# Attention decode and a gated MLP on one core: the scheduler's program against one written out by hand, with 48 KB rows, GpSimd folds and a late output projection

## The chip, the core and the metric

One Trainium2 chip, one of its cores. The metric is device time in microseconds, the median of the runs. The core has TensorE (PE), VectorE (DVE), ScalarE (ACT), GpSimd (POOL) and SyncE (SP), which here only issues DMAs, and 16 DMA engines between HBM and the on-chip memory.

## The reference

One token goes through a layer with a cache of 8192 keys: layernorm, queries of 32 heads of 192, softmax over the scores against K, the sum over V, the output projection, a residual; then layernorm, a gated MLP with ReLU on the gate, and a second residual. All is float32. K and V are 201 MB each, and every element is used once.

```python
q = (layernorm(x) @ wq).reshape(32, 192)             # x: 640
scores = einsum("hd,hkd->hk", q, k_cache) * 192**-0.5  # k_cache: 32 x 8192 x 192
o = einsum("hk,hkd->hd", softmax(scores), v_cache)
h = x + o.reshape(6144) @ wo                          # wo: 6144 x 640
y = layernorm(h)
gate, up = y @ W_gate, y @ W_up                       # 640 x 1536 each
out = h + (gate * (gate > 0) * up) @ W_down           # 1536 x 640
```

## The kernel before, in words

The program is written against a scheduling layer with pools: buffers rotate, and the layer inserts each wait. Every engine still runs its own instructions in the order of the code. SP issues all the large loads, in that order, and a load that must wait for its buffer holds up every load behind it.

- Tiles. The pool `kv` has six buffers of 24 KB per partition (`kv_t`). A head's K (or V) is two of them: `load_kv` (L82) reads half a head, 4096 keys, 32 keys to a partition, one row of 24 KB per partition. At the start five of the buffers hold the slabs of wq, at the end they hold the weights of the MLP.
- Queries. The slabs of wq are multiplied as they land (L159); the result `q4` holds 8 heads side by side on four partitions. `query` (L168) picks one head with the matrix `sel` and spreads it over 128 partitions, in PSUM.
- Scores (`scores_of`). For each 16 keys per partition DVE multiplies K by q in place (L178). DVE sums 10 of the 16 products of 192 (L179), and ACT the other 6, one by one, with an accumulating copy (L181).
- Softmax (`softmax_of`). The maximum goes over PE twice (L189, L193), ACT takes the exponential (L198), PE the sum (L200), DVE its reciprocal.
- Values (`values_of`). 32 matmuls per head (L217), two keys of each partition at a time; they go to four quarters of the output in turn. PE starts on a half as soon as it landed. `ob` (L220) is the scaled copy.
- Output projection. `wo` comes in nine groups (`load_wo`, L90), for four heads each and at the end two: `to_columns` (L232, L235) turns `ob` into columns `oT`, and `output_of` (L241) multiplies the group's rows of wo into the accumulator `acc`, which already holds x.
- Order. The loop at the end of the attention loads K of head h+1 and V of head h in halves, by turns, and issues the scores of h+1 behind the values of h.
- Tail. Behind the last head the weights up, gate and down are loaded in eleven DMAs (L283 to L290), in buffers that K and V left. h, its layernorm, the two projections (`project`, L319), the product and the down projection (L337) follow; the last DMA writes 640 numbers.

Of the kernel before, what the change touches and what calls it, by code (L numbers as in the profile page):

```python
# [1 line left out]

# [5 lines left out]
F32 = mybir.dt.float32  # L8
AF = mybir.ActivationFunctionType
ALU = mybir.AluOpType  # L10
AX = mybir.AxisListType


@with_exitstack
def kernel(
    ctx: ExitStack,
    tc: tile.TileContext,
    x: bass.AP,
    kc: bass.AP,
    vc: bass.AP,  # L20
    wq: bass.AP,
    wo: bass.AP,
    w_gate: bass.AP,
    w_up: bass.AP,
    w_down: bass.AP,
    out: bass.AP,
):
    nc = tc.nc
# [29 lines left out]
    ps_q = ctx.enter_context(tc.tile_pool(name="ps_q", bufs=2, space=bass.MemoryType.PSUM))
    ps_x = ctx.enter_context(tc.tile_pool(name="ps_x", bufs=1, space=bass.MemoryType.PSUM))
    ps_o = ctx.enter_context(tc.tile_pool(name="ps_o", bufs=1, space=bass.MemoryType.PSUM))  # L60
    ps_s = ctx.enter_context(tc.tile_pool(name="ps_s", bufs=2, space=bass.MemoryType.PSUM))
    ps_a = ctx.enter_context(tc.tile_pool(name="ps_a", bufs=1, space=bass.MemoryType.PSUM))

    xT = const.tile([P, DJ], F32, name="xT")
    xrow = const.tile([1, D], F32, name="xrow")
    nc.scalar.dma_start(xT, x[0, 0].rearrange("(p j) -> p j", p=P))
    nc.scalar.dma_start(xrow, x[0])


    wq_v = wq.rearrange("(p j) n -> p j n", p=P)  # L70
    wq_ts = []
    for j in range(DJ):
        t = kv.tile([P, TW], F32, name="kv_t")
        nc.sync.dma_start(t, wq_v[:, j, :])
        wq_ts.append(t)

    def load_kv(src, h, c, parts=1):
        t = kv.tile([P, TW], F32, name="kv_t")
        v = src[h, c * P * R:(c + 1) * P * R, :].rearrange("(p r) d -> p (r d)", p=P)
        n = TW // parts  # L80
        for i in range(parts):
            nc.sync.dma_start(t[:, i * n:(i + 1) * n], v[:, i * n:(i + 1) * n])  # L82
        return t

    def load_wo(gi):
        hs = GROUPS[gi]
        j = len(hs) * DH // P
        t = wts.tile([P, j, D], F32, tag="wo_t", name="wo_t")
        r0 = hs[0] * DH
        nc.sync.dma_start(t, wo[r0:r0 + len(hs) * DH, :].rearrange("(p j) n -> p j n", p=P))  # L90
        return t

    ones = const.tile([P, P], F32, name="ones")
    nc.vector.memset(ones, 1.0)
    eps = const.tile([P, 1], F32, name="eps")
    nc.vector.memset(eps, EPS)
    ident = const.tile([P, P], F32, name="ident")
    from concourse.masks import make_identity
    make_identity(nc, ident)

    sel = const.tile([P, NQ, P], F32, name="sel")
    nc.gpsimd.memset(sel, 0.0)
    for g in range(NQ):
        nc.gpsimd.memset(sel[g * Q:g * Q + 1, g, :], 1.0)

    par = const.tile([P, 2, Q], F32, name="par")
    for i in range(2):
        nc.vector.reduce_sum(par[:, i, 0:1], ident.rearrange("p (g c) -> p g c", c=Q)[:, :, i], axis=AX.X)
        nc.vector.tensor_copy(par[:, i, 1:Q], par[:, i, 0:1].to_broadcast([P, Q - 1]))

    def rstd_of(dst, var, name):

        ve = const.tile([P, 1], F32, name=f"ve{name}")
        nc.vector.tensor_scalar_add(ve, var, EPS)
        sd = const.tile([P, 1], F32, name=f"sd{name}")
        nc.scalar.activation(sd, var, AF.Sqrt, bias=eps)
        y = const.tile([P, 1], F32, name=f"y{name}")
        nc.vector.reciprocal(y, sd)
        t = const.tile([P, 1], F32, name=f"t{name}")
        nc.vector.scalar_tensor_tensor(t, y, ve, y, op0=ALU.mult, op1=ALU.mult)  # L120
        nc.vector.tensor_scalar(t, t, -0.5, 1.5, op0=ALU.mult, op1=ALU.add)
        nc.vector.tensor_mul(dst, y, t)


    s1 = const.tile([P, 1], F32, name="s1")
    nc.vector.reduce_sum(s1, xT, axis=AX.X)
    pm = ps_s.tile([P, 512], F32, name="ps_small")
    nc.tensor.matmul(pm[:, 0:1], ones, s1, start=True, stop=True)
    mean = const.tile([P, 1], F32, name="mean")
# [78 lines left out]
    for po in pos:  # L208
        nc.vector.memset(po, 0.0)
# [159 lines left out]
```

## Time and profile before

| | before |
|---|---|
| median of 3 runs | 1054.98 us (1054.37 to 1055.05) |
| span of the profiled execution | 1052.8 us; it has no other time of its own |
| read from HBM | 445.91 MB, 424 GB/s over the span |
| busy: PE, DVE, ACT, POOL | 438.6, 727.2, 325.1, 1.9 us |
| DMA engines, queue of SP | 99.1% of 16 engines' span, 22472 packets |
| chain that ended last | DMA 65%, DVE 25%, PE 8% |

A time in a view is counted from the span's start. The rows of a timeline give start, length, engine, line and operation, and in brackets the idle time ahead and what ended it. A matmul in float32 stands as two instructions in the trace.

### The profile page before, as it was taken

How to read it: one execution, taken by the hardware profiler on the slowest of the kernel's cores; microseconds unless marked ns; L12 is line 12 of the kernel's file. 1: busy time of each engine (PE TensorE's matmuls, PEld its weight loads, DVE VectorE, ACT ScalarE, POOL GpSimd, SP SyncE). 2: the span in 40 equal slices, each digit the busy share in tenths (PEclk: the TensorE clock that was granted, in tenths of full speed). 3: DMA queues.
4: the chain of work that ended last, by engine and by line, in shares of the span. 5: the costliest groups of instructions: out<-in, count | busy, mean ns of one | idle time of the engine just before them, and what ended most of it. 6: DMA issues, size and time to landing. Idle time of an engine off the chain costs nothing.

```text
span 1052.8 us, 8858 instructions
## 1 busy us (share of the span) xinstructions
PE 438.6 (42%) x3136; PEld 136.1 (13%) x3136; DVE 727.2 (69%) x418; ACT 325.1 (31%) x1676; POOL 1.9 (0%) x11
## 2 busy tenths in 40 slices
PE   3423444344444333433442444344335334432466
PEld 1101111111111010111110111111101111110122
DVE  1188877677867777687776778677876877777641
ACT  0143333223323332232232333233322322333230
POOL 0000000000000000000000000000000000000000
PEclk9756666666666666766666665766667666666667
DMA  9999999999999999999999999999999999999996
GB/s 394 429 429 431 431 427 430 429 431 431 430 430 427 431 430 428 432 429 429 432 430 430 429 430 430 427 431 430 430 425 433 431 430 430 429 430 429 428 421 247
DMA packets 22662, 446.48 MB, mean 424 GB/s; under 512 B 2645, under 2 KB 2649, under 8 KB 4442
## 3 DMA queue, kind: packets, MB, share of 16 engines
q1 hardware_dynamic: 22472, 445.92, 99.1%
q8 instruction: 24, 0.39, 0.2%
q14 instruction: 20, 0.16, 0.0%
q10 hardware_dynamic: 146, 0.01, 0.0%
HBM read 445.91 MB, written 0.00 MB: 424 GB/s over the span
## 4 chain that ended last, share of the span: by engine, by line
DMA 65%; DVE 25%; PE 8%; ACT 1%; issue 1%; SPq 0%
DMA kv_t<-in_A_k_cache_dram 53%; DVE kv_t L178 18%; DMA kv_t<-in_A_v_cache_dram 8%; DVE sc L179 6%; PE po L217 5%; DMA dn_a<-in_B_W_down_dram 2%; DMA kv_t<-in_A_wq_dram 2%; PE q L168 1%; PE ps_small L232 1%; ACT p L198 0%; PE qp L159 0%; PE ps_small L193 0%; PE ps_small L200 0%; DVE oT L235 0%; PE pd L337 0%
## 5 line engine op out<-in xcount | busy, mean ns | idle before, releaser
L178 DVE TENSOR_TENSOR kv_t<-kv_t,q 128x3072 f32<-128x3072 f32 x128 | 423.4, 3349 | 163.4 <-DMA kv_t<-in_A_k_cache_dram 163.0
L181 ACT ACTIVATE kv_t<-kv_t 128x192 f32<-128x192 f32 x768 | 267.6, 349 | 529.5 <-DVE kv_t L178 529.5
L217 PE MATMUL po<-kv_t,p 128*2 128x384 f32 x2048 | 296.0, 747 | 245.6 <-DMA kv_t<-in_A_v_cache_dram 245.6
L179 DVE TENSOR_REDUCE sc<-kv_t 128x10 f32<-128x1920 f32 x128 | 269.1, 2144 | 0.0
L168 PE MATMUL q<-q,sel 128*128 128x192 f32 x64 | 31.0, 589 | 290.4 <-DVE kv_t L178 290.4
L181 ACT ACTIVATION_READ_ACCUMULATOR kv_t<-kv_t 128x1 f32 x768 | 143.3, 187 | 0.0
L217 PEld LDWEIGHTS po<-kv_t,p 128*2 128x2 f32 x2048 | 60.3, 111 | 449.8 <-DMA kv_t<-in_A_v_cache_dram 271.4
L168 PEld LDWEIGHTS q<-q,sel 128*128 128x128 f32 x64 | 15.7, 303 | 319.4 <-DVE kv_t L178 243.0
L220 ACT ACTIVATE ob<-po,rl 128x384 f32<-128x384 f32 x32 | 18.6, 580 | 113.5 <-PE po L217 113.5
L202 DVE RECIPROCAL rl<-ps_small 128x1 f32<-128x1 f32 x32 | 5.4, 168 | 52.6 <-PE ps_small L200 52.6
L191 DVE TENSOR_REDUCE m<-ps_small 1x1 f32<-1x128 f32 x32 | 8.9, 279 | 42.3 <-PE ps_small L189 42.3
L235 DVE STREAM_TRANSPOSE oT<-ps_small 32x192 f32<-32x192 f32 (+1 forms) x32 | 11.8, 367 | 27.1 <-PE ps_small L232 27.1
L232 PE MATMUL ps_small<-ob,par 128*32 128x192 f32 (+1 forms) x144 | 25.7, 315 | 0.7 <-ACT ob L220 0.7
L159 PE MATMUL qp<-kv_t,xn 128*32 128x512 f32 x120 | 19.4, 801 | 10.1 <-DMA kv_t<-in_A_wq_dram 9.1
L200 PE MATMUL ps_small<-rs,ones 128*128 128x1 f32 x64 | 12.4, 264 | 24.9 <-ACT p L198 24.9
L241 PE MATMUL acc<-wo_t,oT 128*32 128x160 f32 (+1 forms) x408 | 19.9, 352 | 4.6 <-DVE oT L235 4.6
L193 PE MATMUL ps_small<-m,ones 1*128 1x1 f32 x64 | 12.3, 259 | 11.9 <-DVE m L191 11.9
L241 PEld LDWEIGHTS acc<-wo_t,oT 128*32 128x32 f32 (+1 forms) x408 | 14.0, 127 | 9.9 <-DVE oT L235 7.8
L200 PEld LDWEIGHTS ps_small<-rs,ones 128*128 128x128 f32 x64 | 9.7, 191 | 27.6 <-ACT p L198 27.6
L193 PEld LDWEIGHTS ps_small<-m,ones 1*128 1x128 f32 x64 | 9.6, 186 | 18.3 <-DVE m L191 18.3
L232 PEld LDWEIGHTS ps_small<-ob,par 128*32 128x32 f32 x144 | 11.3, 109 | 4.8 <-ACT ob L220 1.4
L198 ACT ACTIVATE p<-sc,nb 128x64 f32<-128x64 f32 x32 | 11.1, 348 | 1.2 <-ACT nb L195 0.2
(77 smaller groups left out, 79.9 us busy)
## 6 DMA issues: line engine op xcount, KB each, us to landing
kv_t<-in_A_k_cache_dram SPq DMA_DIRECT2D x64, 3072.0 KB, 33.7
kv_t<-in_A_v_cache_dram SPq DMA_DIRECT2D x63, 3072.0 KB, 39.7
kv_t<-in_A_wq_dram SPq DMA_DIRECT2D x5, 3072.0 KB, 20.7
wo_t<-in_A_wo_dram SPq DMA_DIRECT2D x7, 1920.0 KB, 43.0
kv_t<-in_A_v_cache_dram SPq DMA_DIRECT2D x4, 768.0 KB, 38.3
up_a<-in_B_W_up_dram SPq DMA_DIRECT2D x1, 3072.0 KB, 33.9
gt_a<-in_B_W_gate_dram SPq DMA_DIRECT2D x2, 1536.0 KB, 24.2
wo_t<-in_A_wo_dram SPq DMA_DIRECT2D x2, 960.0 KB, 41.4
```

Of the source, the lines that this page charges most:

```text
L159: nc.tensor.matmul(qps[b][g * Q:(g + 1) * Q, :], xn[:, j:j + 1].to_broadcast([P, Q]), wq_ts[j][:, c0:c0 + QB], start=(j == 0), stop=(j == ...
L168: nc.tensor.matmul(q[:, 0:DH], sel[:, g, :], q4[:, i * DH:(i + 1) * DH], start=True, stop=True)
L178: nc.vector.tensor_mul(ks, ks, q[:, None, :].to_broadcast([P, SUB, DH]))
L179: nc.vector.reduce_sum(sc[:, i0:i0 + SUB - NA], ks[:, :SUB - NA, :], axis=AX.X)
L181: nc.scalar.activation(ks[:, r, :], ks[:, r, :], AF.Copy, accum_out=sc[:, i0 + r:i0 + r + 1])
L193: nc.tensor.matmul(pb[:, 0:1], ones[0:1, :], m1, start=True, stop=True)
L200: nc.tensor.matmul(pl[:, 0:1], ones, rs, start=True, stop=True)
L217: nc.tensor.matmul(po[g * Q:g * Q + 2, :], p[:, 2 * i:2 * i + 2], vts[c][:, r * DH:(r + 2) * DH], start=(i < NQ), stop=(i >= NP - NQ))
L220: nc.scalar.activation(ob, po, AF.Copy, scale=rl)
L232: nc.tensor.matmul(pt[q0:q0 + Q, 0:W], par[:, k, :], ob[:, k * DH + u * W:k * DH + (u + 1) * W], start=(k == 0), stop=(k == 1))
L235: nc.vector.transpose(oT[s], pt[s, 0:W].rearrange("p (c j) -> p j c", c=Q))
L241: nc.tensor.matmul(acc[g * Q:(g + 1) * Q, :], oT[s, j, :], wo_t[s, j, g * DG:(g + 1) * DG], start=False, stop=(last and j == J - 1))
```

## The change

The scheduling layer is gone. Each engine has a list of instructions, with its own semaphores; the waits are written out (`after=`), and a wait is left out where the engine has already seen a later value. The work stays on its engines, with these differences:

- K has two buffers of a whole head (`kt0`, `kt1`), V has one (`vt`), 48 KB per partition each. A load of K or V is one DMA of 128 rows of 48 KB. wq comes in three DMAs into the same buffers.
- V's next load waits for the last value matmul of the head before; K's next load for the last sum of the head two before.
- The scores: DVE multiplies four blocks of 16 keys, GpSimd adds the second half of each product of 192 onto the first as soon as a block is multiplied, DVE then sums the four blocks of 96. ACT no longer sums.
- All queries are spread over the partitions once, at the start (`q_all`, in `zt`); per head ACT copies one into PSUM, two heads ahead.
- The outputs of the heads: per head PE adds `ob` (unscaled) into a row that is the same on all partitions, with the sum of the exponentials beside it, and DVE adds it to `oall` with the mask `ind`, which is 1 on the four partitions of that head. After the last head four instructions with the mask `ind4` make the columns `oT`.
- wo is read in three DMAs (18, 18 and 12 slabs) into `kt0`, `kt1` and `vt`: the first ahead of the last V, the others behind it. Its 192 matmuls come behind the last head. up goes to `zt`, gate to `kt0`, down to `kt1`, each when its buffer is free.

```diff
-    kv = ctx.enter_context(tc.tile_pool(name="kv", bufs=6))
+    kt = [sb(f"kt{i}", P, TW) for i in range(2)]
+    vt = sb("vt", P, TW)
...
+    hw = [load(kt[0].rearrange("p (j n) -> p j n", j=2), wq_v[:, 0:2, :], "k0"),
+          load(kt[1].rearrange("p (j n) -> p j n", j=2), wq_v[:, 2:4, :], "k1"),
+          load(vt[:, 0:H * DH], wq_v[:, 4, :], "w4")]
...
+    pe.op(lambda e: e.transpose(pa[0:1, 0:P], mp, ident), takes=[(to_pe["mp"], 1)], sig=pe.sem)
+    pe.op(lambda e: e.matmul(pb[:, 0:1], ones[0:1, :], m1, start=True, stop=True), takes=[(to_pe["m1"], 1)], sig=pe.sem)
+    pe.op(lambda e: e.matmul(po2[:, DH:DH + 1], ones, rs, start=True, stop=True), takes=[(to_pe["exp"], 1)])
+    for i in range(NP):
+        g = i % NQ
+        pe.op(lambda e, i=i, g=g: e.matmul(po[g * Q:g * Q + 2, :], pr[:, 2 * i:2 * i + 2],
+                                           vt[:, 2 * i * DH:2 * (i + 1) * DH], start=(i < NQ), stop=(i >= NP - NQ)),
+              takes=[(dma_sems["v"], 16)] if i == 0 else [], sig=pe.sem if i == NP - 1 else None)
+    for k in range(2):
+        pe.op(lambda e, k=k: e.matmul(po2[:, 0:DH], par[:, k, :], ob[:, k * DH:(k + 1) * DH],
+                                      start=(k == 0), stop=(k == 1)),
+              takes=[(to_pe["ob"], 1)] if k == 0 else [], sig=pe.sem if k == 1 else None)
...
+    def load_k(h):
+        h_k[h] = load(kt[h % 2], kf[h].rearrange("(p r) d -> p (r d)", p=P), f"k{h % 2}", [h_kfree[h]])
+    def load_v(h):
+        load(vt, vf[h].rearrange("(p r) d -> p (r d)", p=P), "v", [in_loop(h - 1, T_V) if h else h_q[4]])
+    WJ = [0, 18, 36, OJ]
...
+    load_k(0)
+    for h in range(H):
+        if h + 1 < H:
+            load_k(h + 1)
+        else:
+            load_wo(0, h_kfree[H])
+        load_v(h)
+        k3 = kt[h % 2].rearrange("p (r d) -> p r d", d=DH)
+        fold = []
+        for i in range(NSUB):
+            ks = k3[:, i * SUB:(i + 1) * SUB, :]
+            a = dve.op(lambda e, ks=ks, h=h: e.tensor_mul(
+                ks, ks, qb[h % 2][:, None, 0:DH].to_broadcast([P, SUB, DH])), [h_k[h], h_qb[h]])
+            fold.append(pool.op(lambda e, ks=ks: e.tensor_add(ks[:, :, 0:HD], ks[:, :, 0:HD], ks[:, :, HD:DH]), [a]))
+        h_mul3[h] = a
+        for i in range(NSUB):
+            ks = k3[:, i * SUB:(i + 1) * SUB, :]
+            a = dve.op(lambda e, ks=ks, i=i, h=h: e.reduce_sum(sc[h % 2][:, i * SUB:(i + 1) * SUB], ks[:, :, 0:HD],
+                                                               axis=AX.X), [fold[i]])
+        h_kfree[h + 2] = a
...
+            return dve.op(lambda e: e.scalar_tensor_tensor(oall, po2, ind[:, h:h + 1], oall, op0=ALU.mult, op1=ALU.add),
+                          [in_loop(h, T_O), (dve.sem, dve.count)])
...
+        if h + 2 < H:
+            put_q(h + 2, [h_mul3[h]])
+        act.op(lambda e: e.copy(ob, po), [in_loop(h, T_V)], sig=to_pe["ob"])
+    load_wo(1, h_kfree[H + 1])
+    load_wo(2, in_loop(H - 1, T_V))
+    h_up = load(up_t, rows_of(w_up), "up", [h_qb[H - 1]])
...
+    for i in range(3):
+        for j in range(WJ[i], WJ[i + 1]):
+            for g in range(NQ):
+                a = pe.op(lambda e, i=i, j=j, g=g: e.matmul(
+                    acc[g * Q:(g + 1) * Q, :], oT[:, j:j + 1].to_broadcast([P, Q]),
+                    wo_t[i][:, j - WJ[i], g * DG:(g + 1) * DG], start=False, stop=(j == OJ - 1)), [h_oT, h_wo[i]])
+        h_wof.append(a)
+    h_gt = load(gt_t, rows_of(w_gate), "k0", [h_wof[0]])
+    for n, (j0, j1) in enumerate(((0, 6), (6, 9), (9, 10), (10, 11), (11, 12))):
+        a = load(dn_t[:, j0:j1, :], rows_of(w_down)[:, j0:j1, :], f"dn{n}", [h_wof[1]])
```

SP, in the middle of the attention. Before (`kv_t` is a half of K or V; the number tells buffers apart):

```order
L82 DMA kv_t_1321<-in_A_k_cache_dram 128x6144 [waits DMAHW0_49,DVE_49,Activation_49]
L82 DMA kv_t_1323<-in_A_v_cache_dram 128x6144 [waits DMAHW1_49,PE_49]
L82 DMA kv_t_1415<-in_A_k_cache_dram 128x6144 [waits DMAHW2_49,DVE_49,Activation_49]
L82 DMA kv_t_1417<-in_A_v_cache_dram 128x6144 [waits DMAHW3_49,PE_49]
L82 DMA kv_t_1419<-in_A_k_cache_dram 128x6144 [waits DMAHW4_49,DVE_49,Activation_49]
L82 DMA kv_t_1421<-in_A_v_cache_dram 128x6144 [waits DMAHW5_49,PE_49]
L90 DMA wo_t_1537<-in_A_wo_dram 128x3840
```

And now, at the start of the attention, from the first load of the wq slabs:

```order
L137 DMA kt0<-in_A_wq_dram 128x12288
L137 DMA kt1<-in_A_wq_dram 128x12288
L137 DMA vt<-in_A_wq_dram 128x6144
L137 DMA kt0<-in_A_k_cache_dram 128x12288 [waits s_pe]
L137 DMA kt1<-in_A_k_cache_dram 128x12288 [waits s_pe]
L137 DMA vt<-in_A_v_cache_dram 128x12288 [waits s_pe]
L137 DMA kt0<-in_A_k_cache_dram 128x12288 [waits s_dve]
L137 DMA vt<-in_A_v_cache_dram 128x12288 [waits s_pe]
L137 DMA kt1<-in_A_k_cache_dram 128x12288 [waits s_dve]
L137 DMA vt<-in_A_v_cache_dram 128x12288 [waits s_pe]
```

The turns of K and V stay, in pieces twice as long; the waits for two or three engines have become one each, on DVE for K and on PE for V, and wo is gone from between them.

DVE, one head. Before (`kv_t` a half of K, `m1` and `ps_small` the softmax, `oT` the output's columns):

```order
L178 TENSOR_TENSOR kv_t_577<-kv_t_577,q_585 128x3072 [waits DMAHW6_49]
L178 TENSOR_TENSOR kv_t_577<-kv_t_577,q_585 128x3072
L179 TENSOR_REDUCE sc_621<-kv_t_577 128x10 [waits DVE_49] x2
L178 TENSOR_TENSOR kv_t_581<-kv_t_581,q_585 128x3072 [waits DMAHW0_49]
L178 TENSOR_TENSOR kv_t_581<-kv_t_581,q_585 128x3072
L179 TENSOR_REDUCE sc_621<-kv_t_581 128x10 [waits DVE_49] x2
L187 TENSOR_REDUCE mp_654<-sc_621 128x1 [waits DVE_49,Activation_49]
L191 TENSOR_REDUCE m1_658<-ps_small_656 1x1 [waits PE_49]
L202 RECIPROCAL rl_669<-ps_small_667 128x1 [waits PE_49]
L235 STREAM_TRANSPOSE oT_282<-ps_small_671 32x192 [waits PE_49]
```

And now (`bank0` holds q, `bank5` the folded output of the head before, `bank3` the maxima):

```order
L278 TENSOR_TENSOR kt0<-kt0,bank0 128x3072 [waits s_act,dma_k0]
L278 TENSOR_TENSOR kt0<-kt0,bank0 128x3072 x3
L284 TENSOR_REDUCE sc0<-kt0 128x16 [waits s_pool] x4
L287 TENSOR_REDUCE mp<-sc0 128x1 [waits s_dve]
L290 SCALAR_TENSOR_TENSOR oall<-bank5,ind,oall 128x193 [waits s_pe]
L294 TENSOR_REDUCE m1<-bank3 1x1 [waits s_pe]
```

The four multiplies now come first and wait once for the whole head; each sum waits for GpSimd; the gather of the head before stands between the two maxima and waits for PE.

PE, from the last half of the last head's values to the output projection. Before (`po` the values' sums, `par` the matrix that folds them, `acc` the accumulator of the projection):

```order
L217 MATMUL po_221<-kv_t,p 2x384 [waits DMAHW7_49]
L217 MATMUL po_221<-kv_t,p 2x384 x3
L217 MATMUL po_221<-kv_t,p 2x384 [waits DMAHW0_49]
L217 MATMUL po_221<-kv_t,p 2x384 x3
L217 MATMUL po_221<-kv_t,p 2x384 [waits DMAHW1_49]
L217 MATMUL po_221<-kv_t,p 2x384 x3
L217 MATMUL po_221<-kv_t,p 2x384 [waits DMAHW2_49]
L217 MATMUL po_221<-kv_t,p 2x384 x3
L232 MATMUL ps_small<-ob,par 32x96 [waits Activation_49]
L232 MATMUL ps_small<-ob,par 32x96 x3
L241 MATMUL acc<-wo_t,oT 32x160 [waits DVE_49]
L241 MATMUL acc<-wo_t,oT 32x160 x11
```

And now (`vt` is V, and later the last part of wo; `kt` its first two):

```order
L231 MATMUL bank<-vt,pr 2x384 [waits dma_v]
L231 MATMUL bank<-vt,pr 2x384 x31
L235 MATMUL bank<-ob,par 128x192 [waits to_pe_ob]
L235 MATMUL bank<-ob,par 128x192
L326 MATMUL bank<-xrow,ones 32x160 [waits dma_xrow]
L326 MATMUL bank<-xrow,ones 32x160 x3
L332 MATMUL bank<-kt,oT 32x160 [waits dma_k0,s_dve]
L332 MATMUL bank<-kt,oT 32x160 x71
L332 MATMUL bank<-kt,oT 32x160 [waits dma_k1]
L332 MATMUL bank<-kt,oT 32x160 x71
L332 MATMUL bank<-vt,oT 32x160 [waits dma_wo3]
L332 MATMUL bank<-vt,oT 32x160 x47
```

Where 3 slabs of wo (12 matmuls) followed the last V, all 48 (192 matmuls) do, and the last V is waited for in one piece, where it came in a half and four quarters of a half.

More of the change, by code (lines that the diff above doesn't have):

```diff
@@ L93 @@
[L93 to L122, printed above, removed]
@@ L125 @@
[L125 to L129, printed above, removed]
-    nc.vector.tensor_scalar_mul(mean, pm[:, 0:1], 1.0 / D)
-    xc = const.tile([P, DJ], F32, name="xc")
-    nc.vector.tensor_scalar(xc, xT, mean, None, op0=ALU.subtract)
-    xsq = const.tile([P, DJ], F32, name="xsq")
-    nc.vector.tensor_mul(xsq, xc, xc)
@@ L148, with sb, psum @@
[L148 to L154 removed]
+    def sb(name, *shape):
+        return nc.alloc_sbuf_tensor(name, list(shape), F32)[:]
+    def psum(name):
+        return nc.alloc_psum_tensor(name, [P, 512], F32)[:]
+    kt = [sb(f"kt{i}", P, TW) for i in range(2)]
```

480 lines of the change are left out of this document (245 added, 235 removed).

## The prediction

> **What bounds the kernel now.** I read the page first: span, share of each engine, the slices.
>
> ```profile
> span 1052.8 us, 8858 instructions
> PE 438.6 (42%) x3136; PEld 136.1 (13%) x3136; DVE 727.2 (69%) x418; ACT 325.1 (31%) x1676; POOL 1.9 (0%) x11
> DMA  9999999999999999999999999999999999999996
> GB/s 394 429 429 431 431 427 430 429 431 431 430 430 427 431 430 428 432 429 429 432 430 430 429 430 430 427 431 430 430 425 433 431 430 430 429 430 429 428 421 247
> q1 hardware_dynamic: 22472, 445.92, 99.1%
> ```
>
> No engine is full, but DMA is in every slice but the last, at a level 430 GB/s. So the kernel is a stream of 445.92 MB, plus a start (394 in the first slice) and a tail (247 in the last). Next, the DMA view of two stretches of the span: 200 to 480 us, nearly all 24 KB rows, and 1016 to 1036 us, where rows of 6 to 24 KB mix.
>
> ```profile
> q1 hardware_dynamic: 5610, 120.18, 100.2%
> ...
> q1 hardware_dynamic: 899, 8.33, 99.2%
> ```
>
> Columns: packets, MB, share of 16 engines. The first is 280 x 16 x 1.002 = 4489 engine-us, the second 20 x 16 x 0.992 = 317.4. With a cost per byte and one per packet, the two equations give 36.8 us per MB (27.19 GB/s per engine, 435 for sixteen) and 12.3 ns per packet. The packet's price rests on a share printed to a tenth, so 10 to 14 ns is as exact as it is.
>
> What SP waited for, and the chain at the end:
>
> ```profile
> SPq L82 <- DVE sc L179: 830.7, 62, 18.4
> ...
> 1.65 24.09 DMA kv_t<-in_A_wq_dram
> ...
> 983.63 37.41 DMA kv_t<-in_A_v_cache_dram
> 1021.04 0.02 issue
> 1021.05 25.45 DMA dn_a<-in_B_W_down_dram
> 1046.50 0.04 issue
> 1046.55 3.27 PE pd L337 x48
> ```
>
> SP waits 831 us for free K buffers and yet the stream never thins: enough is queued ahead. The stream starts at 1.65 and the down weights that the chain waits for land at 1046.5; three pieces of 320 KB lie behind them, 0.98 MB or 2.3 us, so it ends near 1048.8. The last V lands at 1021.04.
>
> **The change, part by part.**
>
> *Longer rows.* Same bytes. Before: 22472 packets. After: 8192 rows of K and V (48 KB each), 384 of wq, 384 of wo, 896 of the three weights, and 16 for each of 78 DMAs: some 11,100. Saved: 11,360 x 12.3 ns / 16 engines = 8.7 us. Bounds: 0 if a 48 KB row still goes as two packets, 10 if a packet costs 14 ns. I take 8. By the Trainium skill (DMA: Bandwidth & Descriptors, Specifications) line rate needs only 512 B or more, so rows of 24 and 48 KB would be equally fast; the term would be 0, which is the second rival below. The two rows above speak against it.
>
> *Three buffers for six.* K has two tiles of one head, V one. A K or V of 6.29 MB takes 8 x (49152 B / 27.19 + 12) = 14.6 us, a head 29.1. The reload of V waits for the head's last V matmul, and the next K waits behind it on SP. PE rows:
>
> ```profile
> 500.96 5.30 PE L217 MATMUL po<-kv_t,p 128*2 128x384 f32 x32 [7.58 <-DMA kv_t<-in_A_v_cache_dram]
> 1015.67 6.82 PE L217 MATMUL po<-kv_t,p 128*2 128x384 f32 x64
> 0.74 2.81 SPq L74 DMA_DIRECT2D kv_t<-in_A_wq_dram  x5
> ```
>
> Half a head at the half clock is 5.3 us, so a head is at most 10.6; the whole head at 1015.67 took 6.82, warming up on the way. After an idle PE I take 7.1. Issue to first byte is 0.74 to 1.65, about 1 us. So V's next load is queued 8 to 12 us after V landed, while the next K runs for 14.6: no gap, with 3 to 6 us to spare. K's buffer has far more (20 us of work, below, against 43.7).
>
> *Scores.* The multiplies stay, ACT's 768 accumulations go (ACT was idle most of the time, so worth nothing), GpSimd folds each row's 192 products to 96, and DVE then sums all 16 rows of 96, where it summed 10 of 16 rows of 192.
>
> ```profile
> L178 DVE TENSOR_TENSOR kv_t<-kv_t,q 128x3072 f32<-128x3072 f32 x128 | 423.4, 3349 | 163.4 <-DMA kv_t<-in_A_k_cache_dram 163.0
> L179 DVE TENSOR_REDUCE sc<-kv_t 128x10 f32<-128x1920 f32 x128 | 269.1, 2144 | 0.0
> L102 POOL MEMSET sel<- 128x512 f32 x1 | 0.5, 528 | 0.0
> masks.py:199 POOL TENSOR_SCALAR_AFFINE_SELECT ident<-ident 128x128 f32<-128x128 f32 x1 | 0.3, 293 | 0.0
> L355 POOL MEMSET const-float32-0.0<- 128x1 f32 x1 | 0.1, 103 | 0.2 <-issue 0.2
> ```
>
> DVE per head: 4 x 3.35 + 4 x 2.14 x 1536/1920 = 13.4 + 6.9 = 20.3, and about 1 for the maxima and the gather, under 29.1. No row shows a GpSimd add of two inputs. From below, the memset: (528-103)/511 = 0.83 ns an element, 1.4 us for 1536. From above, two full passes of the select at (293-103)/127 = 1.5 ns: 4.7 us. I take the select plus one more read, 2.3 ns, 3.6 us. The last fold ends 3.35 + 4 x 3.6 = 17.8 us after K landed, DVE's three other sums at 18.5: it hides. A head stays under 29.1 while 3.35 + 4 folds + 1.7 + about 2 of softmax does, so up to 5.5 us a fold. By the Trainium skill (GPSIMD Engine Reference, 3.1) an add of 2048 takes 4497 ns against 2293 on the Vector engine, an estimate of 3.4 us here, which it holds to be the wrong engine for it; no row before shows it.
>
> *Query and gather.* ACT copies q into PSUM two heads ahead, in place of a selecting matmul; the gather is one DVE instruction per head. DVE waits there for V's matmuls of the head before, until about 24 us after its K landed, 5 before the next K. Nothing moves.
>
> *Start.* x is read in pieces beside the wq rows:
>
> ```profile
> xT<-in_A_x_dram ACTq DMA_DIRECT2D x1, 2.5 KB, 10.6
> ...
> 15.31 6.96 PE L159 MATMUL qp<-kv_t,xn 128*32 128x512 f32 x48 [1.00 <-DVE par L108]
> ```
>
> Behind rows twice as long it may land at 19 instead of 11, and the first two wq slabs are used up at 31. K's first load waits for that, but the stream gets to it only at 1.65 + 36 = 38. Hidden, by 7 us.
>
> *The tail.* All of wo (15.7 MB) now comes after head 30's K is used; its last 30 of 48 slabs, and up, gate and down, come after the last V: 21.6 MB, 50.7 us by the two prices. And all its matmuls come after V. The rows to cost them:
>
> ```profile
> 186.24 3.29 PE L241 MATMUL acc<-wo_t,oT 128*32 128x160 f32 x48 [0.48 <-DVE oT L235]
> 429.74 1.84 PE L241 MATMUL acc<-wo_t,oT 128*32 128x160 f32 x48 [0.48 <-DVE oT L235]
> 1022.57 0.58 ACT L220 ACTIVATE ob<-po,rl 128x384 f32<-128x384 f32 x1 [7.78 <-PE po L217]
> 1023.20 0.53 PE L232 MATMUL ps_small<-ob,par 128*32 128x96 f32 x8 [0.71 <-ACT ob L220]
> 1024.13 1.02 PE L241 MATMUL acc<-wo_t,oT 64*32 64x160 f32 x24 [0.40 <-DVE oT L235]
> 1028.43 4.71 PE L319 MATMUL pu<-up_a,hc 128*32 128x384 f32 x32 [0.54 <-DMA up_a<-in_B_W_up_dram]
> 1032.96 0.82 PE L319 MATMUL pu<-rest,hc 128*32 128x384 f32 x8
> 1034.00 1.50 PE L319 MATMUL pg<-gt_a,hc 128*32 128x384 f32 x16 [0.22 <-DMA gt_a<-in_B_W_gate_dram]
> 1039.59 0.85 PE L319 MATMUL pg<-rest,hc 128*32 128x384 f32 x8 [0.37 <-DMA rest<-in_B_W_gate_dram]
> 1040.59 0.56 DVE L329 SCALAR_TENSOR_TENSOR gu<-pg,us 128x384 f32<-128x384 f32 x1 [11.35 <-PE pg L319]
> 1042.08 1.39 PE L337 MATMUL pd<-rest,guT 128*32 128x160 f32 x24 [1.63 <-DVE guT L331]
> 1046.55 3.22 PE L337 MATMUL pd<-dn_a,guT 128*32 128x160 f32 x48 [0.51 <-DMA dn_a<-in_B_W_down_dram]
> 1049.84 0.39 DVE L340 SCALAR_TENSOR_TENSOR o<-pd,hr,h 128x160 f32<-128x160 f32 x1 [7.82 <-PE pd L337]
> ```
>
> Six slabs of wo take 3.29 us cold and 1.84 warm. From the last V's landing: V 7.1, copy, fold and oT (about 0.6, 0.6 and seven small DVE instructions that I put at 0.3 each) to 10.5; wo, six slabs cold and 42 warm, 16.2, to 26.7 (its last part lands at 22.8); layernorm to the up projection 3.3 (1025.15 to 1028.43), to 30.0, where up has landed only at 32; 5.3 to 37.3; gate lands at 41.1, and its 5 slabs take between 5 x 0.75 = 3.7 warm and 5.3 cold, 4.8, to 46; gu and its transpose 1.6 (1040.44 to 1042.08), to 47.6; down 12 slabs at 0.54 less what warms up, 5.8, to 53.4; then 3.0 as before (1049.77 to 1052.8): 56.5. The stream alone would give 50.7 + 4 = 55, so the tail is now a chain of PE that just outlasts its loads, where it was a stream. On SP, wo's last part waits for V's matmuls, with up behind it, at 7.1, and the stream needs it at 13.6; gate waits for wo's first 18 slabs, at 17.5, needed at 32; down for the second 18, at 23, needed at 41. None of them thins the stream.
>
> **Sum.** Stream end 1048.8 - 8 = 1040.8; last V at 1040.8 - 50.7 = 990.1; end 990.1 + 56.5 = 1046.6. What lies around the span was 1054.98 - 1052.8 = 2.2 us against the median of the runs (the profiled execution has no time of its own but the span), which I keep: 1048.8 us, 0.6% less.
>
> **The rivals.**
>
> *The long rows bring nothing* (each still moved as two packets, or the price per packet belongs to something else in the small-row stretch). Then the last V lands at 1048.8 - 50.7 = 998.1, the longer tail is still there, and the end is 998.1 + 56.5 + 2.2 = 1056.8: no change that can be told. For it: no row is longer than 24 KB before. Against it: the two rows agree with a constant price.
>
> *The output weights run at the half clock.* 48 slabs x 0.55 = 26.3 us, 10.1 more, of which 2 hide under the wait for up: 1057. For it: the block at 186 us ran cold throughout. Against it: that block is short, and V's 64 matmuls warmed up within 3.5 us.
>
> *GpSimd and DVE hinder each other* (the other side). If a fold and a DVE instruction never overlap, DVE needs 20.3 + 4 x 3.6 + 1.5 = 36 us a head against 29.1, 7 x 32 = 224 us more, 1270. It decides from 5.5 us a fold, or from 2 us of stall per fold. Nothing in the trace excludes it, since GpSimd is idle there. By the Trainium skill (SBUF — State Buffer, Who interferes with whom) a DVE instruction with at most one SBUF input does not contend; the multiply's q is in PSUM and the sum has one input, so by that rule it does not happen.
>
> *One V buffer starves the stream.* If release to first byte took over 14.6 us, each us costs 31 us: 2 us over would be 1111. The PE rows leave 3 us even at the half clock.
>
> **How the numbers follow.** Forecast 0.60, alone 1045 to 1052; rows bring nothing 0.14; cold wo 0.12; GpSimd against DVE 0.08; V starves 0.06. The first three hold 0.86, so the range is 1044 to 1058. About 0.2%, 2.1 us, is what a measurement can tell here. Faster by more: the forecast and a remnant, 0.62; within: most of the two middle cases, 0.20; slower: the last two and the worse end of the middle ones, 0.18.
>
> **What would show it.** Right: some 11,000 packets on q1, GB/s of 432 to 433 in the level slices, POOL's 128 folds near 3.5 us each, DVE waiting for DMA before each head's first multiply, PE's last wo block at 0.31 a slab. Wrong: GB/s dipping once per 29 us (V), DVE waiting for POOL for more than a few us a head, the multiply longer than 3.35, packets near 20,000, or a tail over 60 us behind the last V.

## The result, and the profile after

| | before | after |
|---|---|---|
| median of the runs | 1055.01 us (4 runs, 1054.37 to 1055.08) | 1045.49 us (4 runs, 1044.55 to 1045.86) |
| ratio, 95% interval | | 0.991 (0.9896 to 0.9924) |
| span of the profiled execution | 1052.8 us | 1044.0 us, its own time 1045.73 |

9.5 us faster, 3.3 us under the forecast of 1048.8. The page of the changed kernel, the lines that answer to those shown of before:

```profile
span 1044.0 us, 7181 instructions
PE 362.4 (35%) x3056; PEld 134.7 (13%) x3056; DVE 669.0 (64%) x394; ACT 56.1 (5%) x184; POOL 437.5 (42%) x134
DMA  9999999999999999999999999999999999999997
GB/s 394 443 428 431 438 424 443 428 428 439 430 434 428 434 437 430 428 437 431 432 435 426 438 431 430 433 432 433 433 430 430 431 436 428 426 439 422 428 420 304
q1 hardware_dynamic: 11096, 445.91, 99.2%
q14 instruction: 7, 0.06, 0.0%
```

Still a stream that fills every slice, of the same 445.91 MB, in half as many packets, and at a slightly higher level. The slices now scatter from 422 to 443, since one load is 6 MB; the stretch from 100 to 900 us says it better. Columns of such a row: the stretch, its length, busy time of PE, PE's weight loads, DVE, ACT and POOL with the number of instructions, the granted clock, the share of the DMA engines, GB/s. First before, then after:

```profile
100.00:900.00 800.00, 328.12 (x2257) 99.68 (x2258) 593.35 (x316) 261.41 (x1371) 0.00 (x0) 0.66 1.00 430
```

```profile
100.00:900.00 800.00, 246.95 (x1971) 85.74 (x1971) 568.82 (x302) 35.27 (x135) 378.19 (x111) 0.62 1.00 432
```

430 to 432 GB/s is 0.5%, nearly 5 of some 1000 us. The second line of the page to keep in mind is q14, instructions fetched by DMA: it has 7 packets here, and in the profile of before it had 20:

```profile
q14 instruction: 20, 0.16, 0.0%
```

The groups of the attention after, and what SP waited for:

```profile
L280 POOL TENSOR_TENSOR kt<-kt 128x1536 f32<-128x1536 f32 x128 | 436.8, 3446 | 524.9 <-DVE kt L278 524.9
L278 DVE TENSOR_TENSOR kt<-kt,bank 128x3072 f32<-128x3072 f32 x128 | 420.7, 3349 | 154.6 <-DMA kt<-in_A_k_cache_dram 154.6
L231 PE MATMUL bank<-vt,pr 128*2 128x384 f32 x2048 | 236.4, 630 | 553.3 <-PEq L60 553.3
L284 DVE TENSOR_REDUCE sc<-kt 128x16 f32<-128x1536 f32 x128 | 215.2, 1743 | 0.0
L290 DVE SCALAR_TENSOR_TENSOR oall<-bank,ind,oall 128x193 f32<-128x193 f32 x32 | 13.4, 420 | 134.7 <-PE bank L235 134.7
SPq L137 <- PE bank L231: 891.2, 32, 29.5
```

A fold takes 3.446 us, the multiply 3349 ns as before, to the nanosecond. DVE waits for K's landing, and in the gather for PE's output of the head before, but never for GpSimd. SP's wait for DVE's sums has become one for V's matmuls. PE's idle time stands as "PEq L60", its own sequencer: the hand-written program waits for a landing in an instruction of its own, which the view doesn't follow to the transfer. For the same reason the chain of waits reaches back only 47 us here, and tells nothing of the stream.

One head in the middle, and then the tail:

```profile
508.46 13.15 DVE L278 TENSOR_TENSOR kt<-kt,bank 128x3072 f32<-128x3072 f32 x4 [4.95 <-DMA kt<-in_A_k_cache_dram]
511.90 13.65 POOL L280 TENSOR_TENSOR kt<-kt 128x1536 f32<-128x1536 f32 x4 [16.35 <-DVE kt L278]
521.53 6.73 DVE L284 TENSOR_REDUCE sc<-kt 128x16 f32<-128x1536 f32 x4
523.11 6.84 PE L231 MATMUL bank<-vt,pr 128*2 128x384 f32 x64 [17.92 <-PEq L60]
530.02 0.33 SPq L137 DMA_DIRECT2D vt<-in_A_v_cache_dram  x1
...
988.75 7.82 PE L231 MATMUL bank<-vt,pr 128*2 128x384 f32 x64 [16.02 <-PEq L60]
1000.21 11.66 PE L332 MATMUL bank<-kt,oT 128*32 128x160 f32 x288 [1.65 <-DVE oT L323]
1015.30 1.83 PE L332 MATMUL bank<-vt,oT 128*32 128x160 f32 x47 [1.68 <-issue]
1020.50 5.13 PE L361 MATMUL bank<-zt,hT 128*32 128x384 f32 x40 [1.06 <-DMA zt<-in_B_W_up_dram]
1029.61 5.96 PE L361 MATMUL bank<-kt,hT 128*32 128x384 f32 x40 [3.98 <-DMA kt<-in_B_W_gate_dram]
1035.73 0.56 DVE L371 SCALAR_TENSOR_TENSOR gu<-bank,us 128x384 f32<-128x384 f32 x1 [14.86 <-PE bank L361]
1037.21 3.47 PE L375 MATMUL bank<-kt,guT 128*32 128x160 f32 x96 [1.64 <-DVE guT L372]
1040.83 0.39 DVE L379 SCALAR_TENSOR_TENSOR o<-bank,hr,h 128x160 f32<-128x160 f32 x1 [3.67 <-PE bank L375]
```

V's next load is queued 6.9 us after V landed here. The last V lands at 988.7 (1021.04 before), and from there to the end it is 55.3 us.

The packets themselves, from the records of the trace (no view groups them so):

| | before | after |
|---|---|---|
| last packet of the stream ends | 1048.5 us | 1038.4 us |
| 360 of the 384 last rows, of 2.5 KB, have ended | 1044.4 us | 1037.6 us |
| from the last packet to the end of the span | 4.3 us | 5.5 us |

Before, the last 24 rows come behind a gap of 1.7 us and end one after the other, 0.1 us apart, until 4.0 us behind all others. 24 of 384 is the share of one engine of the sixteen (8 rows of each of three DMAs), so it looks as if one engine were late; the records don't name the engine. The stream ends 10.0 us earlier, of which the longer tail gives back 1.2.

### The profile page after: what moved, and what is told of

Its sections match the earlier page's. It is cut to its first block, busy times and chain, and to the rows that moved or that the text cites. A ratio compares the mean times of both kernels' runs of the same rounds, so it can differ in the third digit from the quotient of the medians.

```text
span 1044.0 us, 7181 instructions
## 1 busy us (share of the span) xinstructions
PE 362.4 (35%) x3056; PEld 134.7 (13%) x3056; DVE 669.0 (64%) x394; ACT 56.1 (5%) x184; POOL 437.5 (42%) x134
## 3 DMA queue, kind: packets, MB, share of 16 engines
q1 hardware_dynamic: 11096, 445.91, 99.2%
HBM read 445.91 MB, written 0.00 MB: 427 GB/s over the span
## 5 line engine op out<-in xcount | busy, mean ns | idle before, releaser
L280 POOL TENSOR_TENSOR kt<-kt 128x1536 f32<-128x1536 f32 x128 | 436.8, 3446 | 524.9 <-DVE kt L278 524.9
L278 DVE TENSOR_TENSOR kt<-kt,bank 128x3072 f32<-128x3072 f32 x128 | 420.7, 3349 | 154.6 <-DMA kt<-in_A_k_cache_dram 154.6
L231 PE MATMUL bank<-vt,pr 128*2 128x384 f32 x2048 | 236.4, 630 | 553.3 <-PEq L60 553.3
L284 DVE TENSOR_REDUCE sc<-kt 128x16 f32<-128x1536 f32 x128 | 215.2, 1743 | 0.0
L231 PEld LDWEIGHTS bank<-vt,pr 128*2 128x2 f32 x2048 | 57.9, 101 | 711.4 <-issue 711.4
L301 ACT COPY ob<-bank 128x384 f32<-128x384 f32 x32 | 15.3, 479 | 805.1 <-PE bank L231 805.1
L235 PE MATMUL bank<-ob,par 128*128 128x192 f32 x128 | 28.4, 345 | 22.4 <-PEq L60 22.4
L235 PEld LDWEIGHTS bank<-ob,par 128*128 128x128 f32 x128 | 19.9, 189 | 44.5 <-issue 44.5
L225 PE MATMUL bank<-rs,ones 128*128 128x1 f32 x64 | 14.9, 302 | 27.7 <-PEq L60 27.7
L211 PE MATMUL bank<-zt,ones 1*128 1x512 f32 x24 | 17.3, 1002 | 0.8 <-ACT zt L199 0.8
```

Of the source, the lines that this page charges most:

```text
L211: a = pe.op(lambda e, g=g, b=b, o=o: e.matmul(o, ones[g * Q:g * Q + 1, :], q4[g * Q:g * Q + 1, b * QB:(b + 1) * QB], start=True, stop=True ...
L225: pe.op(lambda e: e.matmul(po2[:, DH:DH + 1], ones, rs, start=True, stop=True), takes=[(to_pe["exp"], 1)])
L231: pe.op(lambda e, i=i, g=g: e.matmul(po[g * Q:g * Q + 2, :], pr[:, 2 * i:2 * i + 2], vt[:, 2 * i * DH:2 * (i + 1) * DH], start=(i < NQ), s ...
L235: pe.op(lambda e, k=k: e.matmul(po2[:, 0:DH], par[:, k, :], ob[:, k * DH:(k + 1) * DH], start=(k == 0), stop=(k == 1)), takes=[(to_pe["ob" ...
L278: a = dve.op(lambda e, ks=ks, h=h: e.tensor_mul(ks, ks, qb[h % 2][:, None, 0:DH].to_broadcast([P, SUB, DH])), [h_k[h], h_qb[h]])
L280: fold.append(pool.op(lambda e, ks=ks: e.tensor_add(ks[:, :, 0:HD], ks[:, :, 0:HD], ks[:, :, HD:DH]), [a]))
```

## The experiments

Ratios are to the kernel before on the same chip, with the 95% interval. The 9.5 us had to be shared out between the longer rows, ACT's 768 sums, the hand-written waits and the tail.

**1 and 2. Shorter rows in the changed kernel.** K and V in two DMAs of 24 KB rows, as long as before, or in four of 12 KB; all else stays.

```diff
-        h_k[h] = load(kt[h % 2], kf[h].rearrange("(p r) d -> p (r d)", p=P), f"k{h % 2}", [h_kfree[h]])
+        n = TW // 2                                   # or // 4, and range(4)
+        for i in range(2):                            # PE waits for all of V's DMAs
+            h_k[h] = load(kt[h % 2][:, i * n:(i + 1) * n], kf[h].rearrange("(p r) d -> p (r d)", p=P)[:, i * n:(i + 1) * n],
+                          f"k{h % 2}", [h_kfree[h]])     # V alike
```

> The changed kernel, but each load of K and of V is two DMAs of 128 rows of 24 KB instead of one of 48 KB; same buffers, same waits. 8192 data packets and 1024 semaphore packets more. Theory 'price per packet' (10 to 12 ns each, on 16 engines): +5.8 to +7.1 us over the changed kernel's 1045.5, so 1051.2 to 1052.6. Rival 'the gain lies in the waits and in the tail, rows do not matter': 1045.5 within 1 us.

> The changed kernel with each load of K and V in four DMAs of 12 KB rows: 24576 data packets and 3072 semaphore packets more than the changed kernel. Theory 'price per packet': three times the step of the 24 KB rows, +17.3 to +21.3 us, 1063 to 1067. Rival 'rows do not matter': 1045.5 within 1 us. A step that is not three times the first one would speak for another cause, such as the number of DMAs in flight.

Measured: 1049.91 us (0.9954, 0.9942 to 0.9967) and 1059.86 us (1.0051, 1.0039 to 1.0064). The queue's lines of the two:

```profile
q1 hardware_dynamic: 20312, 445.92, 99.4%
```

```profile
q1 hardware_dynamic: 38744, 445.93, 99.6%
```

4.4 us for 9216 more packets and 10.0 for another 18,432: 14.4 x 16 / 27,648 = 8.3 ns of an engine's time per packet, nearly the same in both steps (7.7 and 8.6). These kernels have more DMAs too, but the price shows in the single packets: by the means of the records, two rows of 24 KB take 10.6 ns longer than one of 48 KB, and two of 12 KB 12.1 longer than one of 24 KB, and each row begins some 3 ns before the one ahead of it ends. The long rows are worth something, against the rule of the Trainium skill (DMA: Bandwidth & Descriptors, Specifications) that 512 B is enough for line rate: from 12 to 48 KB it is still 1.4% here. For the change, 11,376 packets x 8.3 / 16 = 5.9 us. The other 3.6 were not accounted for.

**3. The long rows alone, in the kernel before.** Three buffers of 48 KB for six of 24.

```diff
-    R = 32
+    R = 64
...
-    kv = ctx.enter_context(tc.tile_pool(name="kv", bufs=6))
+    kv = ctx.enter_context(tc.tile_pool(name="kv", bufs=3))
...
```

> The kernel before with its scheduler, its ACT sums and its wo groups, but three buffers of 48 KB and K and V in rows of 48 KB (the last V in four pieces of 12 KB, the MLP's weights in three tiles with the same DMAs). Some 8200 data packets and 1000 semaphore packets fewer than before. Theory 'price per packet': 5.8 to 7.1 us less than 1055.0, so 1047.9 to 1049.3, and what is left to 1045.5 belongs to wo, the weights and the end. Rival 'the gain is the late output weights and the hand-written waits': 1055 within 1 us, or more, since three buffers give less lead than six.

Measured: 1052.79 us (0.9983, 0.9974 to 0.9992; 11 runs), only 2.0 faster, with the packets down by 9216 to 13,256, where 8.3 ns each would give 4.8. In the middle it stays at 430 GB/s:

```profile
100.00:900.00 800.00, 277.65 (x2312) 98.16 (x2311) 590.85 (x320) 260.58 (x1365) 0.00 (x0) 0.64 1.00 430
```

So the rows need something else with them, which led to ACT.

**4. Gate in three DMAs**, to take away the wait for gate as a whole in the tail (3.98 us idle and 5.96 cold, above).

```diff
-    h_gt = load(gt_t, rows_of(w_gate), "k0", [h_wof[0]])
+    h_gt = [None] * DJ
+    for n, (j0, j1) in enumerate(((0, 2), (2, 4), (4, 5))):
+        b = load(gt_t[:, j0:j1, :], rows_of(w_gate)[:, j0:j1, :], f"gt{n}", [h_wof[0]])
+        h_gt[j0:j1] = [b] * (j1 - j0)
...
-                                                       start=(j == 0), stop=(j == DJ - 1)), [h_hc, h_w])
+                                                       start=(j == 0), stop=(j == DJ - 1)), [h_hc, h_w[j]])
...
```

> The changed kernel with the gate weights in three DMAs (2, 2 and 1 slabs of five) instead of one, so that PE starts on the gate before all of it has landed. In the trace of the changed kernel PE waits for gate until 1029.6, needs 6.0 us for it at the half clock, and ends the kernel 14.4 us after gate landed while 9.1 us of loads follow it. Theory 'the tail is a chain of PE behind gate': 3 to 4 us less, 1041.5 to 1042.5, until the last piece of the down weights binds. Rival 'the tail is the stream': 1045.5 within 0.5 us.

Measured: 1045.28 us (0.991, 0.9896 to 0.9923): nothing. The timeline's PE rows:

```profile
1029.92 0.85 PE L364 MATMUL bank<-kt,hT 128*32 128x384 f32 x8 [0.40 <-DMA kt<-in_B_W_gate_dram]
1034.61 5.86 PE L378 MATMUL bank<-kt,guT 128*32 128x160 f32 x96 [3.83 <-DMA kt<-in_B_W_down_dram]
```

Gate is done at 1030.8 where it was 1035.6. But the down projection then waits for the landing of its weights, and PE has cooled by then: 5.86 us, at a granted clock of 0.58, for what took 3.47 at 1.00. It ends at 1040.5, where it was 1040.7. My expectation failed: the time went into the next wait.

**5. ACT's instructions back, without their work.** 48 copies of one element per head in the changed kernel, 1536 instructions, as many as ACT's sums were in the trace; nothing reads them.

```diff
+    spare = sb("spare", P, 48 * H)
...
+        for n in range(48):
+            act.op(lambda e, n=h * 48 + n: e.copy(spare[:, n:n + 1], ones[:, 0:1]), [h_ones])
```

> The changed kernel with 48 copies of one element on ACT behind each head's output copy, 1536 instructions whose result nobody reads; ACT's program grows from 184 instructions to about the 1676 of the kernel before, and ACT is still idle most of the time. Theory 'ACT's program is fetched by one DMA engine': the queue q14 has 12 to 13 packets of 8 KB more, 0.31 us each, all on one engine, which ends 3 to 4 us behind the others, as in the kernel before; time 1048.5 to 1049.5. Rival 'the lone late engine came from the buffers' waits or from the rows': 1045.5 within 0.7 us.

Measured: 1049.52 us (0.9952, 0.9939 to 0.9964), 4.0 us slower than the changed kernel.

```profile
q14 instruction: 19, 0.16, 0.0%
```

The stretch from 100 to 900 us is back at 430 GB/s, though these copies don't touch K, V or a buffer that anyone waits for. A fetch of 8 KB on q14 takes 0.31 us in the packet records; 12 more of them, one behind the other on one engine, would be 3.7 us. But that the sizes agree proves little: the row that begins as a fetch ends takes longer as well, by 0.39 us on the mean (0.24 to 0.66), so 12 fetches would come to some 8 us. And the one late engine that I expected didn't come: 360 of the last 384 rows have ended at 1042.4 and the last at 1043.7, 4.8 and 5.3 us later than in the changed kernel. The whole stream is late here; how that follows from a few fetches isn't shown.

**6. The folds in the kernel before**, without ACT's sums; rows, buffers and tail as they were.

```diff
-                nc.vector.reduce_sum(sc[:, i0:i0 + SUB - NA], ks[:, :SUB - NA, :], axis=AX.X)
-                for r in range(SUB - NA, SUB):
-                    nc.scalar.activation(ks[:, r, :], ks[:, r, :], AF.Copy,
-                                         accum_out=sc[:, i0 + r:i0 + r + 1])
+                nc.gpsimd.tensor_add(ks[:, :, 0:DH // 2], ks[:, :, 0:DH // 2], ks[:, :, DH // 2:DH])
+            for r0 in range(0, R, SUB):
+                i0 = c * R + r0
+                nc.vector.reduce_sum(sc[:, i0:i0 + SUB], k3[:, r0:r0 + SUB, 0:DH // 2], axis=AX.X)
```

> The kernel before with GpSimd's folds and DVE's sums of 96 in place of ACT's 768 sums, all else as it was: 24 KB rows, six buffers, the scheduler. ACT's program loses 1536 instructions. Theory 'ACT's program is fetched by one DMA engine': that engine has 3.7 us less to do and the time falls by 3 to 4 us, to 1051 to 1052. Rival 'the folds bring nothing': 1055 within 0.7 us; slower, if DVE (about 24 us of work a head and its waits) becomes the bound.

Measured: 1050.59 us (0.9963, 0.9949 to 0.9976), 4.05 faster than before, with the same rows on q1 and fewer fetches:

```profile
q1 hardware_dynamic: 22472, 445.92, 99.5%
q14 instruction: 10, 0.08, 0.0%
```

The same 4.0 us in the other program and the other direction, with 10 fetches fewer. Here the late engine is gone: 360 of the last rows have ended at 1043.6 and the last at 1044.3, where before it was 1044.4 and 1048.5; in experiment 3, with ACT's sums, 24 rows still come behind a gap, from 1044.1 to 1046.5. That ACT's instructions cost 4 us is shown. That they cost it by their fetch is inferred: from copies that do nothing else, and from the late rows, which in the old program come and go with the sums. That it is their running, or the semaphore that each copy signals, isn't excluded.

**7. Both in the kernel before**, the edits of 3 and 6 together.

> The kernel before with both parts: K and V in 48 KB rows in three buffers (2.0 us less alone) and GpSimd's folds with DVE's sums of 96 in place of ACT's sums (4.1 us less alone); the scheduler, the nine groups of wo and the short tail stay. Theory 'rows and ACT's program add up': 6 us less than 1054.8, 1048.8 within 0.7. Theory 'three buffers in turn starve the stream': no more than the folds alone, 1050.6, or worse. If it reaches 1045.5, the hand-written waits and the late wo bring nothing of their own.

Measured: 1046.72 us (0.9924, 0.9911 to 0.9938), 8.0 faster, more than 2.0 and 4.05 together. The middle runs at 432 GB/s:

```profile
100.00:900.00 800.00, 275.32 (x2255) 97.30 (x2247) 551.29 (x318) 32.18 (x108) 359.95 (x106) 0.64 1.00 432
q1 hardware_dynamic: 13256, 445.92, 99.2%
```

To the changed kernel 1.2 us are left, and (13,256 - 11,096) x 8.3 / 16 = 1.1 of them are packets. So the hand-written waits and the late wo together are worth nothing that can be told. Why the rows alone gave 2.0 isn't settled: with ACT's sums in place a buffer comes free later, and three buffers leave less ahead than six; that is only argued.

**8 and 9. How late may V be queued?** V's reload waits for the next head's maximum on PE, or for the folding of the head's output (`T_O`), instead of the last value matmul (`T_V`).

```diff
-        load(vt, ..., "v", [in_loop(h - 1, T_V) if h else h_q[4]])
+        load(vt, ..., "v", [in_loop(h, T_ALL)] if h else [h_q[4]])          # the first
+        load(vt, ..., "v", [in_loop(h - 1, T_O) if h else h_q[4]])          # the second
```

> The changed kernel with V's next load waiting for the maximum of the next head on PE (3.5 us later than the last value matmul that it waits for now). Theory 'one V buffer has room to spare': the load is queued some 11 to 12 us behind V's landing, the K in flight takes 14.6, so 1045.5 within 1 us. Rival 'the one V buffer is at its limit': each us later costs 31 us, up to 1150.

> The changed kernel with V's next load waiting for the fold of the output on PE (1.5 us later than the last value matmul), so queued some 8.5 us behind V's landing, where 6.9 cost nothing and 10.9 cost 25 us. Theory 'the faster engines run out first, and the loss sets in as soon as the lead falls under their spread': between 1046 and 1055. Theory 'a fixed latency behind the issue is longer than the 1 us that the first load showed, and the loss sets in at once where it is used up': 1045.5 within 0.7.

Measured: 1070.53 us (1.0151, 1.013 to 1.0172; 2 runs) and 1045.86 us (0.9921, 0.9909 to 0.9934; 1045.15 to 1048.87). The first, one head and the stretch:

```profile
503.44 8.15 PE L231 MATMUL bank<-vt,pr 128*2 128x384 f32 x64 [18.05 <-PEq L60]
514.35 0.33 SPq L137 DMA_DIRECT2D vt<-in_A_v_cache_dram  x1
```

```profile
100.00:900.00 800.00, 249.92 (x1926) 83.70 (x1930) 555.77 (x295) 33.96 (x130) 368.26 (x108) 0.61 0.99 420
```

Here V is queued 10.9 us after it landed, with 14.6 us of K in flight from then, and already the stream is thinner: 420 GB/s, 25 us in all, 0.8 a head. The share of the DMA engines tells only a quarter of it (0.99 for 1.00, some 6 us of the 22 that the stretch loses). The rest is in the packets' own records. When V was queued after its landing, over 27 heads, and the mean length in ns of the 48 KB packets by when they begin, in us after that landing:

```
begin after landing   0-9   10    11    12    13    14    15   20-28   V queued after
changed kernel       1823  1832  1818  1821  1819  1825  1819  1819    6.7 to 8.4
second (T_O)         1820  1830  1963  1866  1854  1826  1821  1817    8.2 to 9.9
first (T_ALL)        1819  1852  2185  2156  2178  2015  1926  1819    9.4 to 11.0
```

Packets that begin 11 to 14 us behind the landing, the last one or two that each engine has in flight, take up to a fifth longer when the next load is queued late, though none of their bytes changed; against 1820 ns each that is some 17 us per engine over these heads in the first, and some 4 in the second, whose profiled run was its slowest (1048.87); by its median the second loses nothing that can be told. The margin I gave, to 14.6, ends between 8.4 and 9.5, and the changed kernel stands just within it. Why an engine's last packets need the next load to be known isn't shown.

**10 and 11. The tail warm.** As in 4, with down's first DMA in two and 6 or 3 matmuls that compute nothing behind gate's, to keep PE's clock up.

```diff
...
+    for _ in range(6):                                # or 3
+        pe.op(lambda e: e.matmul(banks[2], ones, zt[:, 0:512], start=True, stop=True))
```

> The kernel with the gate in three pieces, with the down weights' first piece of six slabs cut in two, and six matmuls of 512 columns without use behind the gate's, so that PE's clock is at full when the down weights land. In the kernel with gate in pieces the down block began at 1034.6 and took 5.9 us at the half clock, until 1040.5, while its last piece landed at 1038.7. Theory 'the end is the stream and then a cold PE': 1.0 to 1.6 us less, 1043.7 to 1044.3. Rival 'the end is the stream alone': 1045.3 within 0.4.

> The kernel with gate in three pieces, the down weights' first piece cut in two and three instead of six matmuls without use: six took 5.4 us at the half clock and held the down block up until 1036.4. Three end at about 1033.8, when the first down piece has landed; the block then follows the stream at full clock and ends 0.4 us behind its last piece (1038.6), about 1039.1 instead of 1039.9: 1044.4, 1.1 us less than the changed kernel. Rival 'PE is cold again by then': 1045.3, as with gate in pieces alone.

Measured: 1045.24 us (0.9912, 0.9898 to 0.9925) and 1045.01 us (0.9907, 0.9894 to 0.9921). The first, then the second:

```profile
1031.08 5.42 PE L375 MATMUL bank<-zt,ones 128*128 128x512 f32 x12
1036.42 3.47 PE L380 MATMUL bank<-kt,guT 128*32 128x160 f32 x96
```

```profile
1039.20 0.48 PE L380 MATMUL bank<-kt,guT 128*32 128x160 f32 x8 [0.31 <-DMA kt<-in_B_W_down_dram]
```

Down runs warm now, 3.47 us for 5.86. But six take 5.42 us, at a granted clock of 1.00 (not at half the clock, as I had put it before the second run), and push the down projection back by 1.8 of the 2.4 us that they save. With three, PE waits for the last pieces of down as they land: what is left behind the stream is small. It is the lowest median of all, but 0.5 us under the changed kernel is within the intervals; no version here is shown to beat it.

**12. GpSimd's work doubled**, a second add per fold, whose result nobody reads.

```diff
+            b = pool.op(lambda e, ks=ks: e.tensor_add(ks[:, :, 0:HD], ks[:, :, 0:HD], ks[:, :, HD:DH]), [a])
+            fold.append(pool.op(lambda e, ks=ks: e.tensor_add(ks[:, :, HD:DH], ks[:, :, 0:HD], ks[:, :, HD:DH]), [b]))
```

> The changed kernel with a second add of the same size behind each fold on GpSimd, whose result nobody reads, before DVE may sum: 6.9 us a block instead of 3.45. Theory 'folds are hidden up to 5.5 us a block': the last ends 3.35 + 27.6 us after K landed, then 1.7 of sum and 2 to 2.5 of softmax make 34.7 to 35.2 us a head against 29.1, 5.6 to 6.1 x 31 = 174 to 189 us more, 1219 to 1235. Rival 'GpSimd and DVE already hold each other up': more than that, and the multiplies longer than 3.35 us.

Measured: 1200.15 us (1.1378, 1.1357 to 1.1399; 2 runs), under the 1219 to 1235 expected. Groups of it, and DVE's first multiplies of two heads:

```profile
L278 DVE TENSOR_TENSOR kt<-kt,bank 128x3072 f32<-128x3072 f32 x128 | 419.9, 3334 | 9.5 <-DMA kt<-in_A_k_cache_dram 9.5
L280 POOL TENSOR_TENSOR kt<-kt 128x1536 f32<-128x1536 f32 x128 | 440.4, 3440 | 250.3 <-DVE kt L278 250.3
L281 POOL TENSOR_TENSOR kt<-kt 128x1536 f32<-128x1536 f32 x128 | 439.3, 3432 | 10.0
L285 DVE TENSOR_REDUCE sc<-kt 128x16 f32<-128x1536 f32 x128 | 223.8, 1748 | 410.5 <-POOL kt L281 410.5
...
597.72 13.12 DVE L278 TENSOR_TENSOR kt<-kt,bank 128x3072 f32<-128x3072 f32 x4
631.61 3.33 DVE L278 TENSOR_TENSOR kt<-kt,bank 128x3072 f32<-128x3072 f32 x1
```

DVE now waits for GpSimd, 410 us in all, and no longer for K. From DVE's first multiply of one head to that of the next it is 33.9 us: 3.3 for the first multiply, 27.5 of folds, 1.7 of the last sum leave 1.4 for the maxima and the gather, where 2 to 2.5 were expected. So GpSimd becomes the bound from (29.1 - 6.4) / 4 = 5.7 us a fold; 3.45 is well under it. And with GpSimd never idle for long, neither the multiply nor the fold gets longer: in these instructions the two engines don't hinder each other, as the Trainium skill has it for a DVE instruction with at most one SBUF input (SBUF — State Buffer, Who interferes with whom).

## Why the prediction was right, and where by luck

A gain of 6.2 us was forecast and 9.5 came, inside the range and in the likeliest case. Term by term:

- *Longer rows*: 8 us taken, 5.9 measured. The step that failed is the price of 12.3 ns, taken from the engines' share of two stretches and given as exact to 10 to 14. That share adds up the packets' own times, which overlap (it reads 100.2%): of the 10.6 to 12.1 ns that a row's own time has beyond its bytes, the 3 ns by which it begins before the one ahead ends cost nothing. Changing the rows gives 8.3 ns, with the short packets counted in that signal the end of a DMA. The term's bounds, 0 to 10, covered it.
- *ACT's sums*: "worth nothing", since ACT was idle. Measured 4.0 us, twice. This is the step that was wrong in kind: an idle engine's instructions took nothing from any engine that I looked at, but the stream is the bound, and fetching them seems to take from the stream. The trace had a sign of it in the page's part on the queues, q14 with 20 packets, whose share prints as 0.0%.
- *The fold*: 3.6 us taken, 3.45 measured. The estimate by the Trainium skill (GPSIMD Engine Reference, 3.1), 3.4, was nearer still. At 3.45 it hides, as 12 shows. Whether DVE would have been the better engine no run here tells, since none has DVE sum all.
- *DVE, start, hidden*: 4 x 3.35 + 6.7 = 20 us per head, as predicted (the two rows at 508 and 521); no slice of the stream is thin.
- *V's single buffer*: queued 8 to 12 us after landing predicted, 6.7 to 8.4 measured; no gap, as predicted. But the step "3 to 6 us to spare" failed: the threshold is near 9 us, not 14.6, and less than 1 us is to spare. At the late end of my own 8 to 12 it would have cost 25 us, which I gave 0.06.
- *The tail*: 56.5 us from the last V, 55.3 measured. V 7.8 for 7.1; wo 16.9 for 16.2, with the clock at 0.91 there and a pause of 1.7 us in it that the view can't explain; both hide, since up starts at 31.8 for 32. Gate starts at 40.9 for 41.1. Two sizes were off against each other: gate ran mostly cold (5.96 for 4.8, at a granted clock of 0.57), and down warm (3.47 for 5.8, at 1.00).

```profile
1000.00:1018.00 18.00, 15.55 (x386) 13.97 (x386) 0.49 (x2) 0.40 (x2) 0.00 (x0) 0.91 1.00 427
```

- *A chain of PE that just outlasts its loads*: half right. Experiment 4 took the chain's largest wait away and the loads held the end, within 0.3 us.
- *Around the span*: 2.2 kept, 1.7 measured.

The sum by what was measured: 5.9 + 4.0 = 9.9 of the 10.0 by which the stream ends earlier; less 1.2 for the longer tail, and 0.5 more around the span: 9.2 of 9.5. The share of each depends on the order, since in the old program the rows alone gave 2.0 and both together 8.0. The total came as near as it did by luck: one gain was put 2 us too high, another of 4 us was missed, and the tail was put 1.2 us too long.

Of the rivals, long rows that bring nothing are refuted by 1 and 2; the cold wo by the row above; the hindrance by 12. The starving V is real, and begins less than 1 us behind where the kernel stands.

## What to carry to other kernels

In a kernel that streams at the limit of DMA, count everything that DMA moves, packets and instructions too: price a packet by changing the row length alone, and look at the instruction queues of the page before you call an idle engine's instructions free. A single buffer is enough when its reload is queued well ahead of the end of the transfer in flight; here the lead had to be 5 to 6 us, not zero. And in a tail that ends with its loads, a faster step only moves the wait to the next landing.

## What I had not expected of the hardware

- A DMA packet costs about 8.3 ns of an engine's time beyond its bytes, measured with rows of 12 to 48 KB.
- 1536 more ACT instructions, with 12 more fetches of 8 KB, cost a kernel that is bound by DMA 4.0 us, and as much is gained in the other kernel without them, with 10 fetches fewer. A fetch takes 0.31 us, and the row that begins as it ends takes 0.24 to 0.66 us longer.
- A reload queued 9.4 to 11.0 us after the landing, with 14.6 us of transfers in flight, makes the packets in flight longer (2185 ns for 1820) and costs 0.8 us per head; at 8.2 to 9.9 us, nothing that can be told by the median, and some 3 us in all in its slowest run.
- PE's clock falls within a wait of 4 us: the same 96 instructions took 3.47 us behind 1.64 us of idle time, at a granted clock of 1.00, and 5.86 behind 3.83, at 0.58.
